# One burst for the first two value visits of the last head group, in a one-core attention and gated-MLP kernel

## The chip, the cores and the metric

The kernel runs on one core of a Trainium2 chip. The metric is the device time of one launch in microseconds (us), taken as the median of several runs. The core's engines are TensorE (PE, with its weight loads shown apart as PEld), VectorE (DVE), ScalarE (ACT), GpSimd (POOL) and SyncE (SP, which issues nearly all transfers).

## What is computed

The input x has 2048 tokens of 512 features. One branch is attention with 32 heads of 16 features, in which a token sees itself and the 255 tokens before it; the other is a gated MLP with 1376 hidden features. A sigmoid gate per token mixes them:

```python
q, k, v = (x @ wqkv) split into 32 heads of 16
scores  = q @ k.T * 16 ** -0.5, masked to 0 <= q_index - k_index < 256
a       = softmax(scores) @ v, heads joined, @ wo
b       = (sigmoid(x @ w_gate) * (x @ w_up)) @ w_down
out     = g * a + (1 - g) * b        # g = sigmoid(sum(x * gate_w))
```

All is float32. The large products are made of three products of high and low parts, so nearly every operand is split once: a cast on ACT and a subtraction on DVE.

## The kernel before, in words

**Groups, blocks and steps.** Heads go in 8 groups of 4, tokens in 16 blocks of 128. One step `u` is one block of one group, so that group 7, the last, is u = 112 to 127. The loop over `u` (lines 853 to 1009) runs to 137, since the later stages of a block follow nine and thirteen steps behind. A step is written as four slots, one for each head `hh`. In a slot of step u (lines 910 to 969) these are issued in this order:

- `s_part(u, hh)` (line 360): PE makes the scores of one query block for one head against its three key blocks, in a PSUM bank of the tag `"s"`, of which there are two. DVE then takes their row maximum (line 376, a custom instruction and a read of its accumulator). "Maximum (124, 2)" below is that of u = 124, hh = 2.
- `st_part(u - 9, hh ^ 1)` (line 418): PE makes the transposed scores of a block nine steps back, with the maxima already in the operands, and ACT takes the exponential (line 430) into the probability buffers `pbuf` and `pwide`. POOL clears what the window excludes (`mask_p`).
- a guest from the list `behind`, if there is one and the slot allows it: the low-part subtractions of the weights of the down projection (line 137), each one DVE instruction; and one from `evac` or `acts`, which are mostly copies on ACT.
- `next(slots)`: so many turns of the filler work, which keeps PE busy. One turn is one product of two half-array matmuls running beside each other. The filler is first the gate and up projections (`gu`, line 282), then, from u = 121 on, the tail of them (`tp`, line 612), 16 groups with 12 products each. How many turns a slot has is given by the tables `GAPS` and `GAPS2` (lines 47 and 48): three, or two in the slots that are called dense.

**The tail's end.** When a group of the filler is complete, its `post` is called. For `gu` it is put on the list `evac`. The tail's groups have `None` in the place of what follows (line 684), and for these `post` is called at once, inside the turn:

```python
if behind_it is None:
    post()
else:
    evac.append(lambda behind_it=behind_it, post=post: (post(), behind_it()))
```

That `post` is `tail_post` (line 616): a transpose on DVE from PSUM (line 618) and a copy of one column (line 619). So a tail transpose stands on DVE right behind the slot in which its group ended.

**Value visits.** At some steps PE stops this rhythm for a value visit (`pv_part`, line 451): the products of the probabilities with the values for 512 queries, in 32-column tiles. In the first seven groups two visits go together as one burst every eight steps (`visits[u] == 2`): one in the bank `pv`, which ACT copies out, the second in a bank of the tag `"st"`. The last group has four single visits, at u = 125, 129, 133 and 137 (the table `visits`, line 846). After each visit, at fixed steps, SP is given the loads of sums and of the gate and up results (`SUMS`, `H_LOAD`).

**The maxima's way back.** `max_split` (line 383) makes three small DVE instructions of the maxima of four blocks; they go out to DRAM and back into the operands of `st_part`.

After u = 137 comes the down projection (lines 1059 to 1122), 128 tokens and 11 pieces of hidden features at a time, with the output projection between.

Of the kernel before, what the change touches and what calls it, by code (L numbers as in the profile page):

```python
# [7 lines left out]
F32 = mybir.dt.float32  # L8
# [6 lines left out]
P = 128  # L15
# [7 lines left out]
CH = 512  # L23
NC = T // CH
NB = T // P
# [14 lines left out]
LAG = 9  # L40
PVLAG = LAG + 4
WIDE = 2 * 4
NWIDE = NG - 1
# [3 lines left out]
GAPS = [3] * 12 + [2] * 3  # L47
GAPS2 = [3] * 8 + [2] * 3 + [3] * 10 + [2] * 3 + [3] * 4 + [2] * 3
# [4 lines left out]
TREAD = 133  # L53
WD_LOAD = {119: 0, 120: 1, 121: 2, 122: 3, 128: 4, 129: 5, 131: 6, 132: 7, 135: 8, 136: 9, 137: 10}
WD_SPLIT = {124: 0, 125: 1, 126: 2, 127: 3, 130: 4, 131: 5, 133: 6, 134: 7}
SUMS = {129: 0, 131: 1, 134: 2}
WO = 126
WO_SPLIT = {132: 0, 133: 1, 134: 2, 135: 3}
AHEAD = 7
V_STORE = {2: 0, 3: 1, 6: 2, 10: 3}  # L60
V_LOAD = {122: 7, **{16 * g + 14: g for g in range(7)}}
H_LOAD = {126: (0,), 130: (1, 2), 134: (3, 4), 137: (5, 6)}


@with_exitstack
def gated_mix_kernel(
# [16 lines left out]
    def after(ins, other):  # L83
        tc.add_manual_dep(
            ins.ins, other.ins.name,
            mybir.DependencyInfo(mybir.DependencyClass.Sync, mybir.DependencyReason.DATA), reason="array halves",
        )
# [21 lines left out]
    ps = ctx.enter_context(tc.tile_pool(name="ps", bufs=1, space=PSUM))  # L109
# [11 lines left out]
    NU = NG * NB  # L121
# [18 lines left out]
    behind = []  # L140
# [3 lines left out]
    with ExitStack() as actx:  # L144
# [197 lines left out]
        def run_dmas(dmas):  # L342
            for dst, src in dmas:
                nc.sync.dma_start(dst, src)
# [38 lines left out]
        def max_split(s):  # L383
            mx = mxs.pop(s)
            nm = spool.tile([P, HG, 2, 4], F32R, tag="nm", name=f"nm{s}", bufs=1)
            nc.vector.tensor_scalar(nm[:, :, 0], mx, -1.0, None, op0=ALU.mult)
            nc.vector.scalar_tensor_tensor(
                nm[:, :, 1], mx, -1.0, nm[:, :, 0].bitcast(F32), op0=ALU.mult, op1=ALU.subtract,
            )
            nms[s] = spool.tile([P, QB], F32, tag="nt", name=f"nt{s}", bufs=1)  # L390
            nc.vector.transpose(nms[s], nm.bitcast(F32).rearrange("p h l b -> p (h l b)"))
# [4 lines left out]
        def max_load(s):  # L396
            st = ring[s // 2 % RING].bitcast(F32).rearrange("(a r) j f -> r a j f", r=QB)
            o = s % 2 * CH
            src = max_d[s].rearrange("a (p s) l b t -> p (s l) b a t", p=2)
            for p in range(2):  # L400
                nc.sync.dma_start(
                    st[0, :, p, o:o + CH].rearrange("r (b a t) -> r b a t", b=4, a=P // QB), src[p],
                )
# [1 line left out]
        homes = (((0, 1), (9, 1), (3, 2), (4, 2)), ((0, 1), (3, 1), (9, 2), (10, 2)))  # L405

        def p_home(u):
            if u // NB >= NWIDE:
                return pbuf, *homes[u // 4 % 2][u % 4]
            if u % WIDE < 4:  # L410
                return pbuf, u % 4 * 3, 1
            return pwide, *homes[u // WIDE % 2][u % 4]
# [35 lines left out]
        evac = []  # L448
# [256 lines left out]
        def turns():  # L705
            k3 = 3 * ND
            groups = []
            ended = {}
            sizes = GAPS2 * (NB * NWIDE // WIDE) + GAPS + GAPS[0:12]
            sizes += [6] * 14  # L710
            for size in sizes:
                for _ in range(size):
                    t = turns_done[0]
                    turns_done[0] += 1
                    if t % (3 * k3) == 0 and len(groups) < n_rest:
                        groups.extend((work or rest).pop(0) for _ in range(3))
                    for half, v in enumerate((t, t - SHIFT)):
                        if 0 <= v < n_rest * k3:
                            n, k = divmod(v, k3)
                            n += TURN[half][n % 3] - n % 3  # L720
                            ins = groups[n][0](k, half, n in ended)
                            if k == 0 and n in ended and size > 3:
                                after(ins, exps[ended[n]])
                            if k == k3 - 1:
                                if n not in ended:
                                    ended[n] = len(exps)
                                    continue
                                _, behind_it, post = groups[n]
# [4 lines that stand above are left out]
                yield  # L733
# [108 lines left out]
        def mid(u):  # L842
            return PVLAG <= u < NU and (u - PVLAG) % 4 == 0 and u not in visits

        U_WIDE = NB * NWIDE + LAG
        visits = {u: 2 for u in range(PVLAG + 4, U_WIDE + 1, WIDE)}
        visits.update({u: 1 for u in range(U_WIDE + 4, N, 4)})

# [4 lines left out]
        for u in range(N):  # L853
            if u == LAG:
# [4 lines left out]
                pv = ps.tile([P, CH], F32, tag="pv", name="pv", bufs=1)  # L859
# [50 lines left out]
            for hh in range(HG):  # L910
                wide = visits.get(u) == 2
                if hh == 0 and u in visits:
                    s2 = (u - PVLAG) // 4 - wide
                    pv_part(s2, pv)
                if hh == 3 and mid(u + 1):
                    max_split((u - 4) // 4)
                if hh == 0 and mark:
                    if not mid(u):
                        max_split((u - 5) // 4)
                    run_dmas(later)  # L920
                    later.clear()
                    max_store((u - 5) // 4)
                if hh == 0 and wide:
                    flush(evac)
                    ripe = [held.pop(0) for _ in range(2) if held and held[0] // 2 == u // 8 + 1]
                    for s4 in ripe:
                        proj_hi(s4)
                    o_copy(0, pv)
                    max_load((u - 5) // 4)
                    for s4 in ripe:  # L930
                        proj_lo(s4)
                    run_dmas(later)
                    later.clear()
                    second = ps.tile([P, CH], F32, tag="st", name=f"pv{s2}", bufs=2)
                    pv_part(s2 + 1, second)
                    for guests, n in ((acts, 2), (behind, 3)):
                        for _ in range(min(n, len(guests))):
                            guests.pop(0)()
                    o_copy(1, second)
                    o_store(s2)  # L940
                elif hh == 0 and u in visits:
                    evac.append(lambda s2=s2: o_take(s2, pv))
                if hh == 2 and mark:
                    transfers()
                if u < NU:
                    s_part(u, hh)
                if 0 <= u - LAG < NU:
                    st_part(u - LAG, hh ^ 1 if u < NU else hh)
                if u < LAG:
                    flush(behind)  # L950
                    if hh % 2 == 1:
                        upto = n_first * (2 * u + 1 + hh // 2) // (2 * LAG)
                        run_first(upto - done)
                        done = upto
                else:
                    long = u < U_WIDE
                    k8 = (u - LAG) % WIDE * HG + hh
                    dense = GAPS2[max(0, k8 - 1)] < 3 if long else u < NU and (u - PVLAG) % 4 == 3 and hh > 0
                    k = (u - PVLAG) % 4 * HG + hh
                    free = hh == 2 and not mid(u + 1) if long else k in (1, 5, 9) or k in (3, 7) and len(behind) > 2  # L960
                    if behind and (u < PVLAG or u >= NU or free):
                        behind.pop(0)()
                    if evac:
                        evac.pop(0)()
                    elif acts and not dense and (u < NU or hh % 2 == 1):
                        acts.pop(0)()
                if u >= LAG and (hh % 2 == 1 or u < NU) and (u + 1 not in visits or hh < HG - 1):
                    if u < N - 2:
                        next(slots)
# [17 lines left out]
            if u in WO_SPLIT:  # L987
                acts.extend(lambda d=d: wo_split(d) for d in range(WO_SPLIT[u], WO_SPLIT[u] + 1))
            if u in SUMS:
                sums_load(SUMS[u])  # L990
            if u - 2 in SUMS:
                behind.append(lambda c=SUMS[u - 2]: later.append(sums_invert(c)))
            if u == TREAD:
                tail_reads(0)
            if u >= TREAD:
                tail_read(0, 2)
            for n in H_LOAD.get(u, ()):
                h_load(n)
# [175 lines left out]
```

## Time and profile before

| | |
|---|---|
| median of 3 runs | 720.27 us (719.78 to 720.39) |
| profiled execution, its own time | 718.91 us |
| span in the profile, first to last instruction | 717.2 us |
| PE busy | 711.9 us, 99% |
| PE weight loads busy | 599.9 us, 84% |
| DVE busy | 478.3 us, 67% |
| ACT busy | 430.3 us, 60% |
| POOL busy | 165.6 us, 23% |
| granted TensorE clock | 1.0 (2.4 GHz) |

The shares are means over the whole span. Matmuls overlap and their ends are modelled in the profile, so PE counts as busy also in a short wait between two matmuls. Starts, on the other hand, are recorded. The window of the last group, before its first value visit and after it, is 490 to 516 us; the attention loop ends at 546 us and the down projection takes the rest.

### The profile page before, as it was taken

How to read it: one execution, taken by the hardware profiler on the slowest of the kernel's cores; microseconds unless marked ns; L12 is line 12 of the kernel's file. 1: busy time of each engine (PE TensorE's matmuls, PEld its weight loads, DVE VectorE, ACT ScalarE, POOL GpSimd, SP SyncE). 2: the span in 40 equal slices, each digit the busy share in tenths (PEclk: the TensorE clock that was granted, in tenths of full speed). 3: DMA queues.
4: the chain of work that ended last, by engine and by line, in shares of the span. 5: the costliest groups of instructions: out<-in, count | busy, mean ns of one | idle time of the engine just before them, and what ended most of it. 6: DMA issues, size and time to landing. Idle time of an engine off the chain costs nothing.

```text
span 717.2 us, 17422 instructions
## 1 busy us (share of the span) xinstructions
PE 711.9 (99%) x6298; PEld 599.9 (84%) x6298; DVE 478.3 (67%) x1455; ACT 430.3 (60%) x890; POOL 165.6 (23%) x254
## 2 busy tenths in 40 slices
PE   9999999999999999999999999999999999999997
PEld 7888879888798798988979888798788888888886
DVE  5368767667676676766667667675837767667481
ACT  6423777677576676767667667775576645435341
POOL 5200333233233233323324323232331000000000
PEclk9999999999999999999999999999999999999999
DMA  8466653736456355562655617574568977879531
GB/s 297 121 183 204 212 180 125 221 100 215 156 174 211 106 186 174 172 217 89 214 160 186 195 55 249 180 237 108 166 203 245 252 204 197 211 168 254 144 65 58
DMA packets 102965, 127.20 MB, mean 177 GB/s; under 512 B 45766, under 2 KB 62662, under 8 KB 102880
## 3 DMA queue, kind: packets, MB, share of 16 engines
q1 hardware_dynamic: 102736, 125.98, 57.9%
q8 instruction: 49, 0.80, 0.5%
q14 instruction: 36, 0.29, 0.1%
q10 hardware_dynamic: 144, 0.13, 0.1%
HBM read 71.80 MB, written 51.13 MB: 171 GB/s over the span
## 4 chain that ended last, share of the span: by engine, by line
PE 98%; DMA 1%; SPq 0%; ACT 0%; issue 0%; DVE 0%; DVEq 0%
PE gu L282 28%; PE pj L282 12%; PE pv L460 11%; PE s L370 6%; PE st L425 6%; PE tp L612 6%; PE pd L96 5%; PE pd L94 5%; PE pd L95 5%; PE vh L649 3%; PE pa L94 2%; PE pa L95 2%; PE pa L96 2%; PE vps L511 1%; DMA V<-in_xT_dram 1%; PE pd L1101 1%
## 5 line engine op out<-in xcount | busy, mean ns | idle before, releaser
L376 DVE CUSTOM_DVE_ANT_0 junk<-s,mask 128x384 f32<-128x384 f32 (+2 forms) x512 | 271.4, 530 | 132.9 <-PE s L370 71.8
L282 PE MATMUL gu<-xh,w 64*128 64x512 f32 x1152 | 271.7, 391 | 0.0
L282 PE MATMUL gu<-xl,w 64*128 64x512 f32 x576 | 183.4, 389 | 0.0
L430 ACT ACTIVATE pbuf<-st 128x384 f32<-128x384 f32 (+2 forms) x288 | 138.3, 490 | 61.1 <-PE st L425 30.7
L425 PE MATMUL st<-ring 64*128 64x384 f32 (+2 forms) x536 | 165.8, 326 | 0.0
L370 PE MATMUL s<-ring 64*128 64x384 f32 (+2 forms) x536 | 162.9, 322 | 0.0
L282 PEld LDWEIGHTS gu<-xh,w 64*128 64x128 f32 x1152 | 153.2, 184 | 7.5
L430 ACT ACTIVATE V<-st 128x384 f32<-128x384 f32 (+2 forms) x224 | 100.5, 454 | 47.6 <-PE s L370 25.1
L370 PEld LDWEIGHTS s<-ring 64*128 64x128 f32 x536 | 94.9, 184 | 15.8 <-issue 3.0
L436 POOL TENSOR_SCALAR_AFFINE_SELECT pbuf<-pbuf 128x512 f32<-128x512 f32 x72 | 46.8, 651 | 253.1 <-ACT pbuf L430 198.9
L425 PEld LDWEIGHTS st<-ring 64*128 64x128 f32 x536 | 95.5, 184 | 3.9 <-PE pv L460 0.4
L282 PEld LDWEIGHTS gu<-xl,w 64*128 64x128 f32 x576 | 89.6, 184 | 2.1
L282 PE MATMUL pj<-xl,wqh 64*128 64x512 f32 (+1 forms) x228 | 79.8, 388 | 0.0
L282 PE MATMUL pj<-xh,wqh 64*128 64x512 f32 (+1 forms) x228 | 79.8, 389 | 0.0
L282 PE MATMUL pj<-xh,wql 64*128 64x512 f32 (+1 forms) x228 | 69.7, 389 | 0.0
L95 PE MATMUL pd<-ring,hb 128*128 128x512 f32 x160 | 62.3, 389 | 0.0
L96 PE MATMUL pd<-ring,hb 128*128 128x512 f32 x160 | 62.3, 389 | 0.0
L94 PE MATMUL pd<-ring,hb 128*128 128x512 f32 x160 | 62.3, 389 | 0.0
L436 POOL TENSOR_SCALAR_AFFINE_SELECT V<-V 128x512 f32<-128x512 f32 x56 | 35.8, 640 | 106.8 <-ACT V L430 102.8
L90 ACT CAST hb<-V 128x512 fp32r<-128x512 f32 x40 | 24.9, 622 | 59.3 <-DVE V L812 47.2
L460 PE MATMUL pv<-pbuf,V 128*32 128x384 f32 (+2 forms) x848 | 49.5, 381 | 0.0
L442 POOL TENSOR_SCALAR_AFFINE_SELECT pbuf<-pbuf 128x512 f32<-128x512 f32 x70 | 44.9, 642 | 0.0
(132 smaller groups left out, 1240.4 us busy)
## 6 DMA issues: line engine op xcount, KB each, us to landing
gu_scratch<-sp SPq DMA_DIRECT2D x72, 256.0 KB
V<-gu_scratch SPq DMA_DIRECT2D x36, 512.0 KB
ring<-stack_scratch SPq DMA_DIRECT2D x56, 256.0 KB
stack_scratch<-sh SPq DMA_DIRECT2D x14, 512.0 KB
stack_scratch<-sl SPq DMA_DIRECT2D x14, 512.0 KB
ring<-stack_scratch SPq DMA_DIRECT2D x14, 512.0 KB
guraw<-in_wgu_dram SPq DMA_DIRECT2D x18, 256.0 KB
v_scratch<-V SPq DMA_DIRECT2D x4, 1088.0 KB
```

Source lines behind the costliest of these rows:

```text
L94: mm(ps, lh, rh, start=first, stop=False)
L95: mm(ps, lh, rl, start=False, stop=False)
L96: mm(ps, ll, rh, start=False, stop=last)
L282: return mm(pt, (wl if w == 2 else wh)[r, d], (xl if w == 1 else xh)[r, d, c * CH:(c + 1) * CH], start=k == 0 and not second, stop=k == 3 ...
L370: mm(pt[:, (k - k0) * P:(e - k0) * P], lhsT, blk(g, k, hh, 1, e - k), start=k == k0, stop=e == i + 1, skip_group_check=True,)
L376: nc.vector.tensor_tensor_reduce(junk[:, 0:n], pt[:, 0:n], mask[:, 3 * P - n:], scale=1.0, scalar=NEG, op0=ALU.add, op1=ALU.max, accum_out ...
L425: mm(pt[:, (q - j) * P:(e - j) * P], lhsT, blk(g, q, hh, 0, e - q), start=q == j, stop=e == last, skip_group_check=True,)
L430: exps.append(nc.scalar.activation(p_blk(u, hh, 0, n), pt[:, 0:n * P].rearrange("p (b t) -> p b t", t=P), AF.Exp, scale=SCALE,))
L436: nc.gpsimd.affine_select(buf[:, s0], buf[:, s0], pattern=[[0, HG], [1, P]], compare_op=ALU.is_ge, fill=0.0, base=0, channel_multiplier=-1,)
L442: nc.gpsimd.affine_select(old, old, pattern=[[0, HG], [-1, P]], compare_op=ALU.is_gt, fill=0.0, base=0, channel_multiplier=1,)
L460: mm(bank[32 * hh:32 * hh + w, (q - q0) * P:(e - q0) * P], vt[:, v:v + w], p_blk(g * NB + j, hh, q - j, e - q), start=j == j0, stop=j == q ...
L612: return mm(tp[b][:, 0:TW], (xl if w == 1 else xh)[r, d, b * P:(b + 1) * P], tw[d][int(w == 2)][r, 0:TW], start=k == 0 and not second, sto ...
```

## The change

The bounds `U_WIDE` and `p_home` move by eight steps, so that the visit pattern of the earlier groups goes on until u = 129: the visits of u = 125 and 129 become one burst of two at u = 129, and the probabilities of blocks 112 to 119 lie where those of an earlier group would. The burst's second bank is taken from the tag `"s"`. The turns of the window are dealt by `GAPS2[0:28]` in place of `GAPS + GAPS[0:12]`. A pop from `evac` is skipped in slots with a guest from `behind` and in those ahead of a `max_split`. The loads of sums and of the gate and up results move to steps behind the burst.

```diff
-SUMS = {129: 0, 131: 1, 134: 2}
+SUMS = {130: 0, 132: 1, 134: 2}
...
-H_LOAD = {126: (0,), 130: (1, 2), 134: (3, 4), 137: (5, 6)}
+H_LOAD = {130: (0, 1), 132: (2,), 134: (3, 4), 137: (5, 6)}
...
         def p_home(u):
-            if u // NB >= NWIDE:
+            if u >= NB * NWIDE + WIDE:
                 return pbuf, *homes[u // 4 % 2][u % 4]
...
-            sizes = GAPS2 * (NB * NWIDE // WIDE) + GAPS + GAPS[0:12]
+            sizes = GAPS2 * (NB * NWIDE // WIDE) + GAPS2[0:28]
...
-        U_WIDE = NB * NWIDE + LAG
+        U_WIDE = NB * NWIDE + WIDE + LAG
...
-                    max_load((u - 5) // 4)
+                    if u < NU:
+                        max_load((u - 5) // 4)
...
-                    second = ps.tile([P, CH], F32, tag="st", name=f"pv{s2}", bufs=2)
+                    second = ps.tile([P, CH], F32, tag="st" if u < NU else "s", name=f"pv{s2}", bufs=2)
...
-                    if behind and (u < PVLAG or u >= NU or free):
+                    guest = behind and (u < PVLAG or u >= NU or free)
+                    if guest:
                         behind.pop(0)()
-                    if evac:
+                    if evac and not (NB * NWIDE + LAG <= u < NU and (guest or hh == 3 and mid(u + 1))):
                         evac.pop(0)()
```

The two tables hold the same 78 turns for u = 121 to 127: before 24 slots of three and three of two, now 22 of three and six of two.

On PE, the four slots of u = 124 and the step to u = 125 (`s124_3` is the scores of u = 124, hh = 3; `pv` the visit). Before:

```order
L370 MATMUL s124_3_8488<-ring_63 128x384
L425 MATMUL st115_2_8492<-ring_63 128x384
L460 MATMUL pv_869<-pbuf_868,V_71 32x384 x8
L460 MATMUL pv_869<-pbuf_868,V_71 32x256 x4
L460 MATMUL pv_869<-pbuf_868,V_71 32x128 x4
L370 MATMUL s125_0_8520<-ring_63 128x384
```

And of the change, the same 16 matmuls at u = 129, ahead of the 24 of the next visit:

```order
L425 MATMUL st119_3_8732<-ring_63 128x256
L460 MATMUL pv_869<-pbuf_868,V_71 32x384 x8
L460 MATMUL pv_869<-pbuf_868,V_71 32x256 x4
L460 MATMUL pv_869<-pbuf_868,V_71 32x128 x4
L460 MATMUL pv28_8758<-pbuf_868,V_71 32x128 x4
L460 MATMUL pv28_8758<-pbuf_868,V_71 32x256 x4
L460 MATMUL pv28_8758<-V_71 32x384 x8
L460 MATMUL pv28_8758<-V_71 32x256 x4
L460 MATMUL pv28_8758<-V_71 32x128 x4
L425 MATMUL st120_0_8786<-ring_63 128x384
```

Between the scores of u = 124 and those of u = 125 PE now has filler turns and no visit.

On DVE, around the end of u = 124 (`junk124_3` is maximum (124, 3); `tt1` a tail transpose; `nm30` and `nt30` are `max_split`). Before:

```order
L618 STREAM_TRANSPOSE tt1_8485<-tp1_8342 128x448
L619 COPY gsum_64<-tp1_8342 128x1
L376 ISA junk124_3_8490,mx31_8451<-s124_3_8488,mask_153 128x384
L376 ISA mx31_8451 128x1
L386 TENSOR_SCALAR nm30_8513<-mx30_8157 128x4x4
L387 SCALAR_TENSOR_TENSOR nm30_8513<-mx30_8157,nm30_8513 128x4x4
L391 STREAM_TRANSPOSE nt30_8516<-nm30_8513 128x32
L376 ISA junk125_0_8522,mx31_8451<-s125_0_8520,mask_153 128x384
```

And of the change:

```order
L618 STREAM_TRANSPOSE tt1_8485<-tp1_8342 128x448
L619 COPY gsum_64<-tp1_8342 128x1
L386 TENSOR_SCALAR nm30_8488<-mx30_8157 128x4x4
L387 SCALAR_TENSOR_TENSOR nm30_8488<-mx30_8157,nm30_8488 128x4x4
L391 STREAM_TRANSPOSE nt30_8491<-nm30_8488 128x32
L376 ISA junk124_3_8495,mx31_8445<-s124_3_8493,mask_153 128x384
```

The `max_split` has moved ahead of maximum (124, 3), so that the transpose and the split stand between two neighbouring maxima.

On DVE, the end of u = 125. Of the change:

```order
L376 ISA junk125_2_8546,mx31_8445<-s125_2_8544,mask_153 128x384
L376 ISA mx31_8445 128x1
L137 TENSOR_TENSOR ring_63<-wdraw0_8095,ring_63 128x512
L618 STREAM_TRANSPOSE tt3_8558<-tp3_8403 128x448
L619 COPY gsum_64<-tp3_8403 128x1
L376 ISA junk125_3_8563,mx31_8445<-s125_3_8561,mask_153 128x384
```

The first subtraction of the down weights, which stood behind maximum (126, 1), now stands between the maxima (125, 2) and (125, 3), right ahead of the tail transpose of `tp3`. The transpose of `tp2` stands behind maximum (125, 0), where it stood behind (125, 1). The second and the third subtraction stand behind maximum (126, 2) and (127, 2).

## Rows read from the trace of the kernel before

**Rows 1.** The page: busy time and share of PE and DVE; shares of the chain.

```profile
PE 711.9 (99%) x6298; PEld 599.9 (84%) x6298; DVE 478.3 (67%) x1455; ACT 430.3 (60%) x890; POOL 165.6 (23%) x254
...
PE 98%; DMA 1%; SPq 0%; ACT 0%; issue 0%; DVE 0%; DVEq 0%
```

**Rows 2.** Busy time by engine in a stretch: stretch, length, PE, PEld, DVE, ACT, POOL.

```profile
490.00:514.25 24.25, 24.25 (x256) 21.61 (x253) 19.38 (x68) 16.47 (x35) 7.36 (x12) 1.00 0.51 143
```

**Rows 3.** Waits in 490 to 515 us: total us, times, longest.

```profile
PEld s L370 <- DVE mx L376: 0.6, 2, 0.3
```

**Rows 4.** PE in order of time, a burst of an earlier group: start, us, instruction.

```profile
455.05 2.80 PE L460 MATMUL pv<-pbuf,V 128*32 128x384 f32 x48
...
459.71 0.38 PE L370 MATMUL s<-ring 64*128 64x256 f32 x1
```

**Rows 5.** PE in order of time, the visits at u = 125 and 129.

```profile
501.76 0.39 PE L425 MATMUL st<-ring 64*128 64x384 f32 x1
...
502.08 2.15 PE L460 MATMUL pv<-pbuf,V 128*32 128x384 f32 x32
504.16 0.44 PE L370 MATMUL s<-ring 64*128 64x384 f32 x1
...
504.44 0.36 PE L612 MATMUL tp<-tail_wqh,xh 64*128 64x450 f32 x1
...
516.32 2.80 PE L460 MATMUL pv<-pbuf,V 128*32 128x128 f32 x48
519.05 0.44 PE L425 MATMUL st<-ring 64*128 64x384 f32 x2
```

**Rows 6.** PE in order of time: scores (123, 0), (125, 2), (125, 3), (127, 0), first `st` of u = 128.

```profile
496.86 0.34 PE L370 MATMUL s<-ring 64*128 64x384 f32 x1
...
505.84 0.34 PE L370 MATMUL s<-ring 64*128 64x384 f32 x1
...
506.63 0.34 PE L370 MATMUL s<-ring 64*128 64x384 f32 x1
...
506.81 0.36 PE L612 MATMUL tp<-tail_wqh,xh 64*128 64x450 f32 x1
...
510.90 0.44 PE L370 MATMUL s<-ring 64*128 64x384 f32 x1
...
514.25 0.51 PE L425 MATMUL st<-ring 64*128 64x128 f32 x3
```

**Rows 7.** DVE in order of time, maxima (123, 0) and (123, 1), no guest between them.

```profile
497.50 0.56 DVE L376 CUSTOM_DVE_ANT_0 junk<-s,mask 128x384 f32<-128x384 f32 x1
...
498.21 0.56 DVE L376 CUSTOM_DVE_ANT_0 junk<-s,mask 128x384 f32<-128x384 f32 x1
```

**Rows 8.** DVE in order of time, two maxima with a tail transpose between them (u = 124), and maximum (126, 2).

```profile
501.80 0.56 DVE L376 CUSTOM_DVE_ANT_0 junk<-s,mask 128x384 f32<-128x384 f32 x1
...
502.89 0.54 DVE L376 CUSTOM_DVE_ANT_0 junk<-s,mask 128x384 f32<-128x384 f32 x1
...
510.29 0.55 DVE L376 CUSTOM_DVE_ANT_0 junk<-s,mask 128x384 f32<-128x384 f32 x1
```

**Rows 9.** DVE in order of time, a `max_split` ahead of a maximum (group 6).

```profile
472.06 0.17 DVE L386 TENSOR_SCALAR nm<-mx 128x16 fp32r<-128x16 f32 x1
...
472.61 0.52 DVE L376 CUSTOM_DVE_ANT_0 junk<-s,mask 128x384 f32<-128x384 f32 x1
```

**Rows 10.** DVE in order of time, a subtraction, a transpose and what follows (u = 129).

```profile
516.09 0.65 DVE L137 TENSOR_TENSOR ring<-wdraw,ring 128x512 fp32r<-128x512 f32 x1
516.65 0.64 DVE L618 STREAM_TRANSPOSE tt<-tp 128x448 f32<-128x448 f32 x1
...
517.26 1.07 DVE L137 TENSOR_TENSOR ring<-wdraw,ring 128x512 fp32r<-128x512 f32 x1
```

**Rows 11.** SP and ACT in order of time: the first load of gate and up results, its first reader.

```profile
510.90 1.40 SPq L757 DMA_DIRECT2D V<-gu_scratch x1
...
543.14 0.63 ACT L811 ACTIVATE V<-V 128x512 f32<-128x512 f32 x1
```

## The prediction, made before the changed kernel ran

> **What bounds the kernel now.** I read the page first, for the engines and the chain, and it says TensorE: PE is busy 99% of the span and holds 98% of the chain that ended last, VectorE (DVE) 67% of the span and nothing of the chain [rows 1]. Then I read the stretch that the change touches, from the first slot of the last group to the first of u = 128, 490.00 to 514.25 us. There PE counts as busy all 24.25 us, and DVE 19.38 us, 80% [rows 2]; so PE's busy time doesn't tell whether it waits there. The waits do: the scores' weight loads waited 0.6 us in two cases for a read of DVE's accumulator [rows 3]. A slot's scores need one of two PSUM banks, and get it when the row maximum of two slots before has been read. I read PE and DVE in order of time to see how close the two run.
>
> PE's slot of three turns takes 506.63 - 505.84 = 0.79 us, of which the scores are 506.81 - 506.63 = 0.18 [rows 6]; a turn is then (0.79 - 0.18) / 3 = 0.20, and a dense slot of two turns 0.58. On DVE two maxima in a row start 498.21 - 497.50 = 0.71 apart [rows 7]. So a full slot leaves DVE 0.08 us, and a dense one asks 0.13 more of it than PE gives. Each guest takes it further: with a tail transpose between them two maxima start 502.89 - 501.80 = 1.09 apart [rows 8], 0.38 more.
>
> The Trainium skill (Perfetto Trace Analysis, Identifying the Most-Contended Engine) says that matmul occupancy is a bad measure of how near TensorE is to its limit, and that VectorE's occupancy is a fair one. That speaks against reading the 99% as PE's own work; by the page's view alone the sum would be the first part below and nothing else, -0.4 us, by the skill's it is both parts. The trace bears the skill out in this stretch, in the 0.6 us that PE waited while it was called busy [rows 3].
>
> **Part 1, the merged visits.** No matmul is added or removed: 16 and 24 of the value visits are the same work. What goes is one passage into a visit and one out of it. Alone the visits take 504.16 - 502.08 = 2.08 and 519.05 - 516.32 = 2.73 us, 4.81 together [rows 5]. The same pair as a burst in an earlier group takes 459.71 - 455.05 = 4.66 [rows 4]: 0.15 less. The scores ahead of the visit take 502.08 - 501.76 = 0.32 and those behind it 504.44 - 504.16 = 0.28 [rows 5], against 0.18 inside the rhythm: 0.14 and 0.10 less. Part 1 is -0.39 us. PE is in the chain here, so all of it counts, if nothing else moves.
>
> **Part 2, what the visit at u = 125 gave to DVE.** In its 2.08 us and its passages PE asks nothing of DVE, so DVE catches up there. That break moves out of the window of the maxima, to u = 129, where there are none. The window has the same 28 maxima and the same 78 turns, DVE one guest more (the third subtraction, now ahead of the last maximum), and guests stand in pairs: transpose and `max_split` between the maxima (124, 2) and (124, 3), subtraction and transpose between (125, 2) and (125, 3). The skipped pops don't prevent that: only posts of `gu` and the single visits' copies pass through `evac`, and the tail's transposes are issued inside the turn.
>
> I step through the new order from u = 123 with these prices. A maximum starts 0.71 behind the last [rows 7]; with one guest between, 1.09 [rows 8], also where the guest is a subtraction. A second guest adds, for a transpose and its column copy, 517.26 - 516.65 = 0.61 [rows 10]; for a `max_split`, 472.61 - 472.06 = 0.55 [rows 9]. Scores can start 0.61 behind the start of the maximum two slots before (510.90 - 510.29 [rows 6, 8]). Up to scores (123, 0) at 496.86 [rows 6] and its maximum at 497.50 [rows 7] nothing differs.
>
> - u = 123 is now dense: scores (123, 1) at 497.44, then (123, 2) 498.11 and (123, 3) 498.82, both set by DVE (waits of 0.09 and 0.13). Maximum (124, 2) comes at 497.50 + 6 x 0.71 = 501.76.
> - Transpose and `max_split`: maximum (124, 3) at 501.76 + 1.09 + 0.55 = 503.40. Scores (125, 1) could go at 503.56 by PE and go at 503.40 + 0.61 = 504.01: **wait 0.45**.
> - Maxima (125, 0) 504.11, and behind a transpose (125, 1) 505.20: scores (125, 3), ready on PE at 505.59, go at 505.81: wait 0.22.
> - Maximum (125, 2) 505.91, then subtraction and transpose: (125, 3) at 505.91 + 1.09 + 0.61 = 507.61. Scores (126, 1), ready at 507.39, go at 508.22: **wait 0.83**.
> - u = 126 is dense, and a subtraction stands in it: scores (126, 2), (126, 3) and (127, 0) each wait 0.13, and (127, 1), behind maximum (126, 3) at 510.83, go at 511.44: wait 0.30.
> - Three slots of 0.79 behind that, u = 128 begins at 511.44 + 2.37 = 513.81.
>
> The waits add up to 2.4 us, against 0.6 before [rows 3]. Before, u = 128 began at 514.25 [rows 6], with the visit of u = 125 done. So taking 2.08 us of visit and 0.24 of passages out of the stretch buys only 514.25 - 513.81 = 0.44. At u = 129 the burst of 4.66 stands where 2.73 stood, +1.93. The sum is 1.93 - 0.44 = **+1.5 us**. Ledger by waits as a check: -0.39 + (2.4 - 0.6) = +1.4.
>
> **Edits that I cost at nothing.** The second bank from the tag `"s"`: its last user is the exponential of block 119, hh = 2, and the burst's first visit of 2.08 us [rows 5] lies ahead of it; if that cover is gone, an exponential's wait, some tenths, shows ahead of the second visit. The two banks' copies leave as five larger transfers for ten, and SP's sum load of u = 130 waits for their landing with the loads of the gate and up results behind it: before, the first of those was issued at 510.90 and first read at 543.14 [rows 11]; from u = 130, near 521, it has over 20 us. If that cover is gone, ACT at u = 136 is late, and the down projection behind it. The later subtractions come no later than before. The bounds of the unseen pair of transpose and `max_split`: 0.55 for the split as in [rows 9], which I take since the instructions are the same, or as much as the whole distance of two maxima with a guest, 1.09, which adds 0.5 to the sum; the lower end is 0.38, the price of a first guest, 0.2 less.
>
> **The rivals.** *A, PE's own work alone decides (not slower).* If DVE takes up the guests in the gaps that the 80% leaves it [rows 2], the waits stay at 0.6, and only part 1 is left: 718.91 - 0.39 in the profile, 719.9 us in the median. For it: 20% of the stretch shows DVE idle. Against: 0.71 between maxima with no guest [rows 7] is DVE's pace when it is behind, gaps in it or not. It decides from the pair at the end of u = 125: if the maxima around it stand under 0.9 apart and not 1.70, scores (126, 1) don't wait. The Trainium skill (TensorEngine Tiling (Array Packing), Key Properties) says that a change of tiling mode drains TensorE; by that rule alone the change removes one drain in and one out, which is A, and the passages in [rows 5] agree with it.
>
> *B, the waits reach the tail's banks too.* The transposes of `tp2` and `tp3` end later against PE, and the tail's groups have three banks. By my steps `tp3` is out of its bank near 507.6, and the next group that wants one begins in the slot of (126, 1), at 508.4. If DVE is over 0.8 us later than I have it, PE waits for that too; another 0.5 to 1.0 us, 722.3 to 722.8. Nothing in the waits of before shows it.
>
> *C, half of it.* The transposes wait for nothing, pairs cost less than two guests, and DVE keeps up in u = 126: the two waits of 0.45 and 0.83 alone, halved, give -0.39 + 0.6 and about 720.5.
>
> **How the numbers follow.** The profiled execution took 718.91 us, the median of the runs is 720.27, 1.36 more; I add the sum to the median: 720.27 + 1.5 = **721.8 us**. A measurement of this kernel can tell about 0.2% from no change, 1.44 us, so the likeliest time lies right at that bound. Chances: the forecast, 721.2 to 722.3, 0.55; A 0.15; B 0.15; C 0.15. Two in three of the forecast's 0.55 and all of B are above 721.7, so slower 0.50; faster than 718.8 would need A and a gain that no row shows, 0.05; the rest, 0.45, within 0.2%. The range runs from A's 719.9 to B's 722.8.
>
> **What would show it.** In the profile after: the burst at u = 129 of 4.66 us; scores (125, 1), (126, 1) and (127, 1) starting 1.1 to 1.6 us behind the scores before them, or with slots well over 0.8; more and longer waits of scores' weight loads on DVE than 0.6 us; u = 128 beginning near 513.8. From there to the end all runs 1.9 later. If slots of 125 to 127 keep 0.79 us and u = 128 begins near 512, the steps on DVE are wrong and A holds.

## The result, and the profile after

The changed kernel takes 722.48 us (median of 10 runs, 720.79 to 725.36), the kernel before 720.27 in as many (719.25 to 724.36): a ratio of 1.0032 with a 95% interval of 1.0019 to 1.0044. It is slower by 2.2 us; 1.5 were forecast, and the interval, 1.4 to 3.2 us, holds both. The profiled execution took 721.92 us, of which the span is 719.3 (before 718.91 and 717.2), so 2.1 us of their difference are in the span. The page after:

```profile
PE 712.4 (99%) x6298; PEld 601.6 (84%) x6298; DVE 478.2 (66%) x1455; ACT 430.8 (60%) x890; POOL 164.3 (23%) x254
...
PE 98%; DMA 1%; DVE 1%; SPq 0%; issue 0%; ACT 0%; DVEq 0%
```

Against [rows 1] the shares differ in DVE's alone: 66% busy for 67, and 1% of the chain for 0. The place is found by starts on PE. I measure from the start of the burst at u = 121 to the start of the visit at u = 137, cut where u = 128 begins, and call the pieces the window and the tail. Ahead of it the two profiles agree (the burst begins at 484.52 after, 484.68 before), and from its end to the end of the span both take 174 us. Busy time in the two pieces, before (stretch, length, PE, PEld, DVE, ...):

```profile
484.68:514.25 29.57, 29.57 (x350) 24.49 (x349) 20.78 (x75) 17.34 (x37) 7.99 (x13) 1.00 0.43 118
514.25:543.23 28.98, 28.98 (x313) 24.61 (x310) 16.33 (x36) 21.18 (x50) 12.45 (x18) 1.00 0.69 202
```

And after, with the stretch of [rows 2] ahead:

```profile
490.00:514.35 24.35, 23.12 (x220) 19.94 (x221) 20.03 (x68) 16.34 (x34) 7.33 (x12) 1.00 0.51 151
484.52:514.35 29.83, 28.60 (x318) 22.99 (x317) 21.41 (x75) 17.23 (x36) 7.96 (x13) 1.00 0.42 124
514.35:545.19 30.84, 30.84 (x344) 25.49 (x342) 14.64 (x35) 21.69 (x51) 11.14 (x18) 1.00 0.62 172
```

The window lost a visit of 2.08 us and its passages and is 0.26 longer; the tail took the visit in and is 1.86 longer. Together 60.67 for 58.55: +2.12, which is the whole difference of the spans. PE's row now shows 1.23 us idle in the window, where before it showed none. The waits in 490 to 515 us after, which answer to [rows 3]:

```profile
PEld s L370 <- DVE mx L376: 3.9, 10, 1.1
...
PE s L370 <- DVE mx L376: 1.2, 2, 0.7
```

PE in order of time after: scores (125, 0), (125, 1), (125, 3), (126, 1) and (127, 1), the beginning of u = 128, and the burst with what follows it.

```profile
502.71 0.34 PE L370 MATMUL s<-ring 64*128 64x384 f32 x1
504.37 0.44 PE L370 MATMUL s<-ring 64*128 64x384 f32 x1 [0.69 <-DVE mx L376]
...
506.17 0.44 PE L370 MATMUL s<-ring 64*128 64x384 f32 x1
...
508.57 0.44 PE L370 MATMUL s<-ring 64*128 64x384 f32 x1 [0.55 <-DVE mx L376]
...
511.77 0.44 PE L370 MATMUL s<-ring 64*128 64x384 f32 x1
...
514.35 0.43 PE L425 MATMUL st<-ring 64*128 64x128 f32 x3
...
516.33 2.80 PE L460 MATMUL pv<-pbuf,V 128*32 128x384 f32 x48
518.95 2.12 PE L460 MATMUL pv<-V 128*32 128x384 f32 x32
521.00 0.44 PE L425 MATMUL st<-ring 64*128 64x384 f32 x2
```

The burst takes 4.67, as in [rows 4]. Scores (125, 1) stand 1.66 behind the scores ahead of them, where a slot is 0.79. What DVE (and POOL) did ahead of them, in order of time; 501.60 is maximum (124, 2) and 503.79 maximum (124, 3):

```profile
501.60 0.56 DVE L376 CUSTOM_DVE_ANT_0 junk<-s,mask 128x384 f32<-128x384 f32 x1
...
502.19 0.65 DVE L618 STREAM_TRANSPOSE tt<-tp 128x448 f32<-128x448 f32 x1
...
502.96 0.63 POOL L436 TENSOR_SCALAR_AFFINE_SELECT pbuf<-pbuf 128x512 f32<-128x512 f32 x1 [1.94 <-PE tp L612]
...
503.00 0.62 DVE L387 SCALAR_TENSOR_TENSOR nm<-mx,nm 128x16 fp32r<-128x16 f32 x1
...
503.55 0.63 POOL L442 TENSOR_SCALAR_AFFINE_SELECT pbuf<-pbuf 128x512 f32<-128x512 f32 x1
...
503.79 0.52 DVE L376 CUSTOM_DVE_ANT_0 junk<-s,mask 128x384 f32<-128x384 f32 x1
```

The two maxima stand 2.19 apart; 1.64 were forecast. One instruction of `max_split`, line 387, took 0.62 us. The line's own row says that this is not its price (count: minimum, median, maximum in ns):

```profile
L387 DVE SCALAR_TENSOR_TENSOR nm<-mx,nm x32: 174/175/625, 52.0 to 515.8; 128x16 fp32r<-128x16 f32 x32
```

### The profile page after: what moved, and what is told of

It is laid out like the page before. It is cut to its first block, busy times and chain, and to the rows that moved or that the text cites. A ratio compares the mean times of both kernels' runs of the same rounds, so it can differ in the third digit from the quotient of the medians.

```text
span 719.3 us, 17415 instructions
## 1 busy us (share of the span) xinstructions
PE 712.4 (99%) x6298; PEld 601.6 (84%) x6298; DVE 478.2 (66%) x1455; ACT 430.8 (60%) x890; POOL 164.3 (23%) x254
## 4 chain that ended last, share of the span: by engine, by line
PE 98%; DMA 1%; DVE 1%; SPq 0%; issue 0%; ACT 0%; DVEq 0%
PE gu L282 27%; PE pj L282 13%; PE pv L460 11%; PE s L370 6%; PE st L425 6%; PE tp L612 5%; PE pd L94 5%; PE pd L95 5%; PE pd L96 5%; PE vh L649 3%; PE pa L94 2%; PE pa L96 2%; PE pa L95 2%; PE vps L511 1%; DMA V<-in_xT_dram 1%; PE pd L1103 1%
## 5 line engine op out<-in xcount | busy, mean ns | idle before, releaser
L430 ACT ACTIVATE pbuf<-st 128x384 f32<-128x384 f32 (+2 forms) x272 | 130.4, 490 | 54.5 <-PE st L425 28.4
L430 ACT ACTIVATE V<-st 128x384 f32<-128x384 f32 (+2 forms) x240 | 108.2, 456 | 52.7 <-PE s L370 26.5
L436 POOL TENSOR_SCALAR_AFFINE_SELECT pbuf<-pbuf 128x512 f32<-128x512 f32 x68 | 43.4, 639 | 246.8 <-ACT pbuf L430 228.0
L436 POOL TENSOR_SCALAR_AFFINE_SELECT V<-V 128x512 f32<-128x512 f32 x60 | 38.4, 639 | 116.1 <-ACT V L430 112.1
L460 PE MATMUL pv<-pbuf,V 128*32 128x384 f32 (+2 forms) x800 | 46.7, 381 | 0.0
L282 PEld LDWEIGHTS pj<-xh,wql 64*128 64x128 f32 (+1 forms) x228 | 41.4, 185 | 1.7
```

Source lines behind the costliest of these rows:

```text
L282: return mm(pt, (wl if w == 2 else wh)[r, d], (xl if w == 1 else xh)[r, d, c * CH:(c + 1) * CH], start=k == 0 and not second, stop=k == 3 ...
L430: exps.append(nc.scalar.activation(p_blk(u, hh, 0, n), pt[:, 0:n * P].rearrange("p (b t) -> p b t", t=P), AF.Exp, scale=SCALE,))
L436: nc.gpsimd.affine_select(buf[:, s0], buf[:, s0], pattern=[[0, HG], [1, P]], compare_op=ALU.is_ge, fill=0.0, base=0, channel_multiplier=-1,)
L460: mm(bank[32 * hh:32 * hh + w, (q - q0) * P:(e - q0) * P], vt[:, v:v + w], p_blk(g * NB + j, hh, q - j, e - q), start=j == j0, stop=j == q ...
```

## The experiments

My theory: PE waits in the window for the row maxima, since DVE has lost the break that the visit at u = 125 was; the 0.62 us come from POOL's clear of a window beside it. The rivals: the time is PE's own (order of products, longer burst), or it goes to the tail's banks or transfers. The program ahead of u = 121 is the same in all these kernels, but the stretch from 424 to 456 us, where PE in some executions waits for maxima coming back from DRAM, took from 30.4 to 34.7 us in the profiles; so the pieces of the trace below are read from u = 121 on, and the medians only with their intervals. Each ratio is to runs of the kernel before that were made beside (medians 719.67 us for e1 to e4, 719.94 for e5 to e8, 719.36 for e9 to e12), so a median of an experiment isn't to be compared with 720.27. Of a kernel that ran once only the trace is used.

| kernel | window | tail | both | median us (runs) | ratio to before, 95% |
|---|---|---|---|---|---|
| before | 29.57 | 28.98 | 58.55 | 720.27 (10) | |
| change | 29.83 | 30.84 | 60.67 | 722.48 (10) | 1.0019 to 1.0044 |
| e1, change, narrow maxima | 27.49 | 30.83 | 58.32 | 720.47 (10) | 0.9996 to 1.0024 |
| e2, before, narrow maxima | 29.13 | 28.96 | 58.09 | 719.03 (10) | 0.9982 to 1.0001 |
| e3, split behind the maximum | 29.72 | 30.83 | 60.55 | 723.05 (4) | 1.0031 to 1.0066 |
| e4, subtractions late | 28.93 | 30.88 | 59.81 | 722.19 (6) | 1.0024 to 1.0049 |
| e5, clears late | 29.84 | 30.83 | 60.67 | 721.30 (1) | |
| e6, transposes deferred | 28.96 | 31.22 | 60.18 | 724.54 (1) | |
| e7, 84 turns, subtractions late | 28.84 | 30.59 | 59.43 | 720.83 (12) | 1.0008 to 1.0029 |
| e8, before, subtractions late | 29.40 | 28.95 | 58.35 | 719.37 (12) | 0.9989 to 1.0006 |
| e9, no clear of block 115 | 29.38 | 30.84 | 60.22 | 721.71 (1) | |
| e10, narrow maxima, no guests | 27.37 | 30.82 | 58.19 | 719.82 (1) | |
| e11, 84 turns, last slot empty | 28.85 | 30.49 | 59.34 | 721.11 (11) | 1.0009 to 1.0032 |
| e12, 87 turns, last slot empty | 29.05 | 31.92 | 60.97 | 722.07 (6) | 1.0026 to 1.0051 |

**Is it DVE? (e1, e2).** The maxima of u = 121 to 127 shortened, in the change and in the kernel before:

```diff
-            n = (i + 1 - k0) * P
+            n, w = (i + 1 - k0) * P, P if u >= NB * NWIDE + LAG else (i + 1 - k0) * P
...
-                junk[:, 0:n], pt[:, 0:n], mask[:, 3 * P - n:], scale=1.0, scalar=NEG,
+                junk[:, 0:w], pt[:, n - w:n], mask[:, 3 * P - w:], scale=1.0, scalar=NEG,
```

> This kernel leaves out part of the row maxima of the last group: from u = 121 on each maximum reads 128 columns in place of 384. Theory (VectorE's pace sets the window of u = 121 to 127): with narrow maxima no scores wait for a bank, u = 128 begins some 21.3 us behind the burst at u = 121 in place of 24.5, and the span falls by about 3.1 us, to 716.2. Rival (the 2.1 us come from the burst at u = 129, its second bank or the later loads): the span stays within 0.5 us of 719.3, and the loss shows behind 514 us.

> The kernel before, with the same maxima left out in part (128 of 384 columns from u = 121 on). Theory: only the 0.6 to 0.8 us of waits before goes, span near 716.5; so with narrow maxima the change is the faster one, by the 0.39 us of the merged visits (in the profile; too small for the times). Rival: the change stays slower than this by about 2 us.

Busy time in the window, of e1 and then of e2 (DVE is the third engine):

```profile
485.90:513.39 27.49, 27.10 (x319) 23.85 (x318) 14.52 (x77) 17.04 (x36) 7.96 (x13) 1.00 0.45 135
```

```profile
485.00:514.13 29.13, 29.13 (x351) 24.74 (x349) 14.41 (x76) 17.36 (x37) 7.96 (x13) 1.00 0.38 105
```

With the same matmuls, the change gets 2.35 us shorter and the kernel before 0.46. The +2.12 of the change shrinks to +0.23, so at least 1.9 of it is DVE's pace and not PE's order of products. Of e1 one wait is left, at scores (125, 1); that is taken up in e10. The span that I had expected was missed by 2.1 us in e1: the two pieces fell by 2.35 where 3.1 were expected, and the stretch from 424 to 456 us alone took 1.1 more than in the change. In e2 it was missed by 0.5.

**The split put back (e3).**

```diff
-            return PVLAG <= u < NU and (u - PVLAG) % 4 == 0 and u not in visits
+            return PVLAG <= u < NU and (u - PVLAG) % 4 == 0 and u not in visits and u != U_WIDE - 4
```

> The change with its max_split of u = 124 put back to where it stood, behind maximum (124, 3), so that it is no longer in one gap with a tail transpose. The pair took 2.19 us from maximum to maximum in the change, and was put at 1.64. Theory: a transpose alone is 0.38 beyond the pace and the split alone 0.33 to 0.7, so the maxima behind come 0.4 to 0.8 us earlier and so does u = 128; span 718.5 to 718.9. Rival (the waits are PE's own or come from the tail's banks): no change.

0.12 less, where 0.4 to 0.8 were expected. Behind maximum (124, 3) the split met the clears all the same: line 386 took 0.33 and line 387 0.55 us beside them. So moving it by one maximum avoids nothing, and the run doesn't part order from clear.

**The subtractions taken out of the window (e4; e8 in the kernel before).**

```diff
-                    free = hh == 2 and not mid(u + 1) if long else k in (1, 5, 9) or k in (3, 7) and len(behind) > 2
+                    free = not NB * NWIDE + LAG <= u < NU and hh == 2 and not mid(u + 1) if long else k in (1, 5, 9) or k in (3, 7) and len(behind) > 2
```

> The change with the three low-part subtractions held back to u = 128 and later. Theory: 0.60 (the one in a pair with a transpose) and 0.38 go from VectorE's chain ahead of maximum (126, 3), so u = 128 begins about 0.9 us earlier, span 718.4; the third subtraction, behind the maximum that sets the last wait, is worth nothing. Rival (the tail's banks or the dense slots set the waits): under 0.2 us.

> The kernel before with its two subtractions of the window held back to u = 128. Theory: the two waits behind them fall away (0.2 to 0.4 us), from the burst to the last visit 58.2 to 58.4 against 58.55; in time no difference that can be measured. Rival (VectorE has slack in the kernel before): nothing falls.

```profile
485.13:514.06 28.93, 28.27 (x319) 23.09 (x317) 20.20 (x73) 17.14 (x36) 7.96 (x13) 1.00 0.43 128
```

The window of e4 is 0.90 shorter, as expected, the tail nearly the same: the three subtractions cost the change 0.86 us. The kernel before has two in its window, and they cost 0.20 (e8, as expected); there they stand behind the visit, each alone between two maxima. Which of these makes the difference no run shows. The median of e4 doesn't show the gain: by the trace it should be 1.0018 of before, and its interval begins at 1.0024. With one profile of it I can't say where the rest lies; in that profile 0.75 us of it are in the stretch from 424 to 456.

**The clear (e5, e9).** In e5 the clears were issued later in the program:

```diff
-                mask_p(u - LAG)
+                for v in {123: (), 124: (), 125: (114, 115, 116)}.get(u, (u - LAG,)):
+                    mask_p(v)
```

> The change with GpSimd's clears of blocks 114 and 115 issued one and two steps later, behind u = 125. In the change one 128x16 instruction of max_split at u = 124 took 0.63 us while such a clear ran, against 0.17 to 0.18 in the 30 of 32 splits where none ran beside it. Theory (GpSimd's clear held it up): it takes 0.18 again, maxima (124, 2) and (124, 3) stand 1.7 to 1.8 apart in place of 2.19, and the time from the burst at u = 121 to the last visit falls from 60.67 by 0.4 us. Rival (the split is slow because it stands behind a transpose): it still takes 0.5 or more, and nothing falls.

The order on POOL stayed what it was: the clear still stood beside line 387, which took 0.63 us. It tested nothing, but repeats the change: 60.67 again. So in e9 the clears of one block were left out:

```diff
-            if 0 <= u - LAG < NU:
+            if 0 <= u - LAG < NU and u - LAG != NB * NWIDE + 3:
```

> The change without GpSimd's two clears of block 115 (this leaves out a part of the window's mask). In the change these ran from 502.96 to 504.19 us, and the second instruction of max_split, on 128x16 elements, took 0.63 us from 503.00 on. The run with late clears left them where they were, and the instruction at 0.63. Theory (VectorE and GpSimd get in each other's way there): 0.18 us now, maxima (124, 2) and (124, 3) about 1.75 apart in place of 2.19, from the burst at u = 121 to the last visit 60.2 in place of 60.67. Rival (its place behind a transpose and a column copy makes it slow): still above 0.5, 60.67.

DVE in order of time in e9, maximum (124, 2), line 387 and maximum (124, 3):

```profile
502.63 0.56 DVE L376 CUSTOM_DVE_ANT_0 junk<-s,mask 128x384 f32<-128x384 f32 x1
...
504.05 0.17 DVE L387 SCALAR_TENSOR_TENSOR nm<-mx,nm 128x16 fp32r<-128x16 f32 x1
...
504.39 0.52 DVE L376 CUSTOM_DVE_ANT_0 junk<-s,mask 128x384 f32<-128x384 f32 x1
```

Line 387 is back at 0.17, the maxima stand 1.76 apart (1.75 expected), and both pieces together take 60.22 (60.2 expected). The clear beside the split costs the change 0.45 us.

**No guests, narrow maxima (e10).** The edits of e1, e3 and e4 together.

> The change with maxima of 128 columns from u = 121 on (this leaves out a part of the maxima), and with its max_split put back behind maximum (124, 3) and the subtractions late, so that no wait for VectorE should be left. Theory: then the merged visits alone are left of the change: 58.09 of the kernel before with narrow maxima, less 0.39 and less 0.1 of waits it still had: 57.6 to 57.7 from the burst at u = 121 to the last visit. Rival (the burst of the last group costs something of its own): 58.1 or more.

It came out at 58.19, on the rival's side: 0.10 above e2, not 0.4 below. But the burst took 4.67 us, as in the change and in [rows 4], so it costs nothing of its own. The slot ahead of scores (125, 2) still held 0.38 too much and the passage behind it 0.10. DVE and POOL there:

```profile
503.74 0.63 POOL L436 TENSOR_SCALAR_AFFINE_SELECT pbuf<-pbuf 128x512 f32<-128x512 f32 x1 [1.95 <-PE tp L612]
...
503.82 0.57 DVE L386 TENSOR_SCALAR nm<-mx 128x16 fp32r<-128x16 f32 x1
...
504.32 0.63 POOL L442 TENSOR_SCALAR_AFFINE_SELECT pbuf<-pbuf 128x512 f32<-128x512 f32 x1
504.43 0.55 DVE L387 SCALAR_TENSOR_TENSOR nm<-mx,nm 128x16 fp32r<-128x16 f32 x1
```

Both instructions of the split met a clear, and took 1.12 us where 0.35 are their price. Less those 0.48 it would be 57.7, where the theory had it. In e1 the slot ahead of scores (125, 1) and the passage behind it held 0.66 too much, and 58.32 less those is 57.7 as well. Both are worked out, and no run has both the clear and the guests away.

**The transposes handed to `evac` (e6).**

```diff
-            (lambda k, h=None, x=False, b=b: tail_mm(b, k, h, x), None, lambda b=b: tail_post(b)) for b in range(NB)
+            (lambda k, h=None, x=False, b=b: tail_mm(b, k, h, x), lambda: None, lambda b=b: tail_post(b)) for b in range(NB)
```

> The change with the tail's transposes really sent through the list evac, so that the new guard applies to them: none stands in one gap with a subtraction or a max_split, and each comes a slot later. Theory (VectorE's chain): the chain ahead of maximum (126, 3) gets 0.7 to 1.4 us shorter, but a tail bank is then read up to a slot later than PE wants it, which shows as waits of tail matmuls for the gsum copy, up to 1 us in all; from burst to last visit 60.4, give or take 0.6. Rival (pairs of guests alone are what costs): 59.3 or less, no waits on gsum.

Now the skipped pops do move the transposes, and 0.49 is gained, within what was expected. The waits of e6 from u = 121 to 520 us:

```profile
PEld s L370 <- DVE mx L376: 1.6, 5, 0.5
PEld tp L612 <- DVE gsum L619: 1.0, 1, 1.0
```

The waits for maxima shrink from 3.9 to 1.6, and a new one appears: the filler waits for a tail bank whose transpose is late. That is my rival B's wait; in e1, e5 and e9 it is 0.2 us, and in the change there is none.

**More filler in the window (e7, e11, e12).** All with the subtractions late, so that they stand against e4; e7, e11 and e12 in this order:

```diff
-            sizes = GAPS2 * (NB * NWIDE // WIDE) + GAPS2[0:28]
-            sizes += [6] * 14
+            sizes = GAPS2 * (NB * NWIDE // WIDE) + [3] * 28
+            sizes += [6] * 8 + [5] * 6
...
+            sizes += [6] * 13 + [0]
...
+            sizes = GAPS2 * (NB * NWIDE // WIDE) + [3] * 16 + [4] * 3 + [3] * 9
+            sizes += [6] * 12 + [3, 0]
```

> The change with three turns in all 28 slots of the window (84 in place of 78, six slots behind u = 128 with five in place of six) and the three subtractions held back to u = 128. Theory: what PE waits for VectorE is filled with work that is otherwise done later, the chain loses 0.98, and u = 128 begins 12.5 to 13.5 us before... in numbers: from the burst at u = 121 to the last visit 57.9 to 58.5 us, against 60.67 for the change and 58.55 for the kernel before, so about as fast as the kernel before or up to 0.1% faster. Rival (dense slots help PE in some way): no better than the change with late subtractions, 59.8.

> As the kernel with 84 turns and late subtractions, but the six turns are taken from the last slot of u = 135, which is then empty, so that no slot has five (there, tail matmuls waited 1.0 us for exponentials). Theory: 59.43 less 0.7 to 1.0: 58.4 to 58.7 from the burst at u = 121 to the last visit, level with the kernel before (58.55). Rival (the waits for exponentials stay with fewer turns behind the window): 59.2 or more.

> The same with 87 turns in the window, four in the slots where PE still waited (u = 125, hh = 0 to 2), and nine fewer behind it. Theory: about 0.6 us of waits is filled with turns that are otherwise done later: 57.9 to 58.3, some 0.3 to 0.6 us under the kernel before, at the edge of what the times can tell. Rival: VectorE's chain grows by what a transpose that now ends earlier takes (0.38 us), and nothing is gained over the run with 84.

Busy time in the window and the tail, and the waits in both, of e7:

```profile
485.65:514.49 28.84, 28.81 (x331) 24.73 (x330) 19.95 (x75) 17.02 (x36) 7.99 (x13) 1.00 0.43 129
514.49:545.08 30.59, 30.19 (x333) 24.17 (x330) 16.45 (x35) 21.57 (x51) 12.06 (x18) 1.00 0.60 171
...
PEld s L370 <- DVE mx L376: 1.1, 3, 0.4
PEld tp L612 <- ACT pbuf L430: 1.0, 2, 0.8
```

And of e12:

```profile
485.81:514.86 29.05, 29.05 (x336) 25.58 (x335) 20.18 (x75) 17.02 (x36) 7.96 (x13) 1.00 0.41 128
514.86:546.78 31.92, 31.05 (x326) 24.33 (x323) 16.89 (x36) 21.46 (x50) 12.07 (x18) 1.00 0.62 173
...
PEld tp L612 <- ACT pbuf L430: 1.7, 5, 0.8
```

In the window this goes as expected: six turns more, 1.2 us of work, cost nothing (e7 is 0.09 under e4), as they fill PE's waits. In e12, with nine more, no wait for a maximum is left; less those nine turns of 0.20 its window would be 27.25, which is the window of before less the visit and its passages (29.57 - 2.32); of e2's window, where no maximum is waited for, 26.81 would be left. So the change's window of 29.83 holds 2.6 to 3.0 us that aren't PE's work. Both pieces together miss what was expected in all three; e11 comes out on its rival's side. The misses are in the tail: with fewer turns a slot there is too short for ACT's exponentials, and PE waits for those. Six turns fewer should take 1.2 off and take 0.3 to 0.4 off, and in e12 the tail gets longer. No version of the change that leaves nothing out beat the kernel before; the best, e11, stands at 59.34 us, 0.8 above it.

## Why the prediction was right, and where its size was off

**The bound.** Right: DVE's maxima bound the window once the break is gone. Forecast +1.5, measured +2.1 in the span and +2.2 in the medians, within the range. That the range reached so far was in part luck: 722.48 lies just above the forecast's own 721.2 to 722.3, in the stretch that I had given to rival B, and B's wait didn't come.

**Part 1.** The burst took 4.67 for 4.66, and the tail 1.86 more for 1.93. The gain of the passages in the window stands in no run by itself; it can be worked out where DVE is nearly out of the way, from e10 and e1.

**Part 2, step by step.** Distances between starts of scores, as forecast and in the trace after:

| from, to | forecast | measured |
|---|---|---|
| (123, 0) to (123, 3) | 1.96 | 2.03 |
| (123, 3) to (125, 1) | 5.19 | 5.65 |
| (125, 1) to (125, 3) | 1.80 | 1.80 |
| (125, 3) to (126, 1) | 2.41 | 2.40 |
| (126, 1) to (127, 1) | 3.22 | 3.20 |
| (127, 1) to u = 128 | 2.37 | 2.58 |

Four of six steps hold to 0.07, the pair of subtraction and transpose between the maxima (125, 2) and (125, 3) among them. **The term that was mis-sized is transpose and `max_split` between the maxima (124, 2) and (124, 3):** 1.64 forecast, 2.19 measured, 0.55 more (in the table 0.46, as 0.09 of the same step went the other way). 0.43 of it is the clear: without it 1.76 is left (e9), 0.12 above my price. I had named an upper bound of that size for the split but took 0.55 "since the instructions are the same"; what stands beside them on POOL wasn't the same. The trace of before held the warning: there line 387 took up to 0.48 us, at 503.57, beside a clear, and so did my own [rows 10], where I used the start of the subtraction at 517.26 and not its 1.07 us. The other 0.21 are the last three slots, where I counted 0.79 each and they took 0.90, 0.83 and 0.85: at u = 127 a slot has three starts of scores and `st`, not two, and the first came behind a wait. Before, the same slots took 0.83, 0.79 and 0.84, which could have been read.

**The edits costed at nothing** cost nothing: no wait stands ahead of the burst's second visit, and in the tail PE's waits are those for issue and one of 0.2 us behind a visit. The skipped pops did nothing for the transposes, as said; e6 shows what they would do.

**The rivals.** A falls by e1 and e2. B's wait for the tail's banks isn't among the waits after. C's halved waits fall by the table; the waits were longer, not shorter.

## What to carry to other kernels

When work is taken out of a stretch on the engine that is called the bound, step through the second engine's new order there, instruction by instruction, since 80% busy left no room for pairs of guests. Measure from start to start: PE counted as busy 99% of the span while the window held at least 2.6 us of lost time. And price an instruction by its longest case as well as its median, and look at what another engine does beside that case.

## What the hardware showed that I had not expected

A small DVE instruction waited out a whole POOL instruction. Line 387, with two inputs from SBUF, takes 0.174 to 0.18 us in 31 of its 32 cases, before and after; in the one that began while a clear ran it took 0.62 (before 0.48) and ended 0.02 to 0.03 us behind the clear's end. The subtraction of 1.07 us in [rows 10], also with two inputs from SBUF, began at 517.26 beside a clear, and the next clear, which began while it ran, was held in its turn. POOL there, before:

```profile
517.16 0.63 POOL L436 TENSOR_SCALAR_AFFINE_SELECT pbuf<-pbuf 128x512 f32<-128x512 f32 x1 [1.48 <-ACT pbuf L430]
517.74 1.08 POOL L442 TENSOR_SCALAR_AFFINE_SELECT pbuf<-pbuf 128x512 f32<-128x512 f32 x1
```

Line 386 has one input from SBUF and was held too: of the seven cases that began beside a clear after the change, six took 0.23 to 0.40 us in place of 0.17. The maxima weren't touched: 190 of them began beside a POOL instruction after the change, with the same median of 0.56 as the other 322. The Trainium skill (SBUF — State Buffer, SBUF: two separate sides) says that VectorE and GpSimd share one pair of ports under an exclusive lock, which a VectorE operation needs when it is in a 2-port performance mode, or has two SBUF inputs while the GpSimd operation reads SBUF, and that the loser stands still for the whole instruction. The ends in these traces, the held clear and e9 agree with it, and so does that the maxima, which read one of their inputs from PSUM, were free. In which mode line 386 ran no run here shows.

The scores behind a wait also took a longer passage, 0.28 us to the next filler product in place of 0.18, and such a slot took 0.90 (504.37 to 505.27) in place of 0.79; no view of waits counts these 0.10 us.

Last, the stretch between the visits near 424 and 456 us, which no edit touches, took 30.4 us in the profiles of both kernels and up to 34.7 in e6, where this stands among PE's waits:

```profile
PE st L425 <- DMA ring<-max_scratch: 2.5, 1, 2.5
```

Why that transfer comes late in some executions stays open. Less this stretch, the window and the tail, the spans of the 14 profiles are 627.9 to 629.0 us, so most of what else differs between them lies here; I take it for the reason why a difference of 1 us between two medians isn't resolved, which no run shows.
